# k transposed on VectorE with SBUF transfers in place of TensorE, and seven products reordered in halves of PSUM banks (RWKV-6 attention followed by a GELU MLP)

## The chip, the cores and the metric

One core of a Trainium2 chip. The metric is device microseconds (us) of one execution. A kernel's runs agree within about 0.3% where nothing else is said. In the profile, PE is TensorE's matmuls, PEld its weight loads, DVE is VectorE, ACT ScalarE, SP SyncE; a "q" behind the name is that engine's sequencer, which also issues transfers.

## The reference

```python
# attention: r, k, v, w of (4 batches, 8 heads, 768 steps, 48), u of (8, 48), all float32
for t in range(S):
    cur = u * k[t] (outer) v[t]
    y[t] = r[t] @ (state + cur)
    state = w[t][:, None] * state + k[t] (outer) v[t]
# then, over 3072 rows of 384:
h = x @ w_in                 # 384 x 2048
g = 0.5 * h * (1 + erf(h / sqrt(2)))
out = g @ w_out              # 2048 x 384
```

## The kernel before

The rows are worked through in eight tiles of 384. The MLP of one tile runs on PE while DVE and ACT prepare the attention of the next; attention and MLP are written as generators, and a list says after which step of the MLP each slot of the attention is emitted, which fixes the order on every engine:

```python
    for x in range(1, NX):
        place = ([...] if x == 1 else
                 [0, 1, 4, 10, 14, 16, 17, 18, 20, 22])
        ...
        for step, _ in enumerate(mlp(x - 1)):
            ...
            while place and place[0] <= step:
                place.pop(0)
                next(slots)
```

Three slots of the attention matter. First k, with channels in the partitions and positions in columns, is scaled by DVE (the last of "quarters"). kv needs it the other way round. So it is transposed on PE and copied from PSUM by ACT; then it is the stationary operand (the weights) of 96 small matmuls, "kv", the chunk states:

```python
        for b in range(np_):
            kt_ps = ps.tile([128, 2, BANK], F32, name="kt_ps", tag="d", bufs=3)
            for i in range(NI):
                o = (i % N3) * 128
                nc.tensor.transpose(kt_ps[:, i // N3, o:o + 128], k[:, (b * NI + i) * 128:(b * NI + i + 1) * 128], ident)
            kt = kx[...].rearrange("p (i g d) -> p i g d", g=2, d=G)
            nc.scalar.copy(out=kt.rearrange(...), in_=kt_ps[:, :, 0:N3 * 128])
            kts.append(kt)
        yield
        ...
                        nc.tensor.matmul(kv_ps[half[g], p, i * D:(i + 1) * D], lhsT=kts[b][half[p], i, g, :],
                                         rhs=vs(b, i, g)[half[p], 0:D], start=True, stop=True)
```

On the MLP's side, the second layer is done in seven products of half blocks (16 steps, in place of eight), each of eight matmuls of 192 columns that the trace counts as 16. The first leaves p1, which four others need:

```python
            o1, o2 = psum(), psum()                          # a bank each, two banks in all
            product(o1, of_blocks(0, 0), of_w(0, 0), True)
            nc.scalar.copy(out=p1, in_=o1)
            yield                                            # here: the transposes of k
            product(o1, of_blocks(0, 1), of_w(1, 0))         # goes on adding into o1
            nc.scalar.copy(out=o_sb[0][:, 0:HM], in_=o1)
            yield                                            # here: kv
            product(o2, of_sums(s2), of_t(1), True)
            nc.vector.tensor_add(u2, o2, p1)
            yield
            # ... four more products
```

Of the kernel before, what the change touches and what calls it, by code (L numbers as in the profile page):

```python
# [10 lines left out]
F32 = mybir.dt.float32  # L11
# [10 lines left out]
G = 64  # L22
D = 48
T = 384
Q = 2
NC = T // C
N3 = NC // 2
NI = Q * N3
LEVELS = (1, 2, 4, 8, 16, 32)
QUARTERS = (1, 4, 16)  # L30
BANK = 512
PIECE = 768
AHEAD = 5
SHARES = 8
HALFWAY = 2


# [5 lines left out]
def kernel(  # L43
# [25 lines left out]
    nc = tc.nc  # L69
# [16 lines left out]
    ps = ctx.enter_context(tc.tile_pool(name="ps", bufs=1, space=PSUM))  # L86
# [186 lines left out]
    def attention(x, unit):  # L273
# [6 lines left out]
        n_u = qs * T  # L280
# [50 lines left out]
        def halves():  # L331

            for h in LEVELS:
# [27 lines left out]
                    copy_diagonal(diag)  # L361
                yield

        def quarters():



            n_c = 2 * NI * np_
            rx = kx.rearrange("p (n x) -> p n x", n=n_c)

            def views(h):
                m = C // 4 // h
                r4 = r.rearrange("p (n m four j) -> p n m four j", m=m, four=4, j=h)
                t4 = tot[h].rearrange("p (n m four) -> p n m four", m=m, four=4)
                ends = (0, 3 * C // 4, 5 * C // 4, 6 * C // 4)
                return m, r4, t4, *(rx[:, :, i:j].rearrange("p n (m x) -> p n m x", m=m) for i, j in zip(ends, ends[1:]))

            def plain(h):
                m, r4, t4, s0, s1, s2 = views(h)
                for z, f in ((s0[:, :, :, 0:h], 1), (s1[:, :, :, 0:h], 2), (s2, 3)):  # L380
                    nc.scalar.copy(out=z, in_=r4[:, :, :, f, :])  # L381

            def lay_out(h):
                m, r4, t4, s0, s1, s2 = views(h)
                z = s1[:, :, :, h:]
                nc.vector.tensor_mul(z, r4[:, :, :, 3, :], t4[:, :, :, 2:3].to_broadcast(z.shape))
                nc.vector.tensor_mul(s0[:, :, :, h:], s1, t4[:, :, :, 1:2].to_broadcast(s1.shape))

            diag = diagonal()
            plain(1)  # L390
            lay_out(1)
            copy_diagonal(diag)
            yield
            for h in QUARTERS:
                m, r4, t4, s0, s1, s2 = views(h)
                ds = []
                for n in range(0, np_ * NI, 4):
                    d = ps.tile([128, 2, BANK], F32, name="d", tag="d", bufs=3)
                    for i in range(4):
                        for g in range(2):  # L400
                            for p in range(2):
                                nc.tensor.matmul(d[half[p], g, i * 3 * C // 2:(i + 1) * 3 * C // 2],  # L402
                                                 lhsT=kc[half[g], (n + i) // NI, (n + i) % NI, p],
                                                 rhs=rx[half[g], 2 * (n + i) + p], start=True, stop=True)
                    ds.append(d[:, :, 0:4 * 3 * C // 2].rearrange("p g (n x) -> p g n x", n=4))
                z = r4[:, :, :, 1:, :].rearrange("p n m b j -> p n m (b j)")
                nc.vector.tensor_mul(z, s0, t4[:, :, :, 0:1].to_broadcast(z.shape))
                if h < QUARTERS[-1]:
                    plain(4 * h)
                k4 = k.rearrange("p (n four j) -> p n four j", four=4, j=h)  # L410
                z = k4[:, :, 0:2, :].rearrange("p n b j -> p n (b j)")
                t2 = tot[2 * h].rearrange("p (n two) -> p n two", two=2)
                nc.vector.tensor_mul(z, z, t2[:, :, 1:2].to_broadcast(z.shape))  # L413
                z = k4.rearrange("p n (b two) j -> p n b two j", two=2)[:, :, :, 0, :]
                tz = t4.rearrange("p n m (b two) -> p (n m) b two", two=2)[:, :, :, 1:2]
                nc.vector.tensor_mul(z, z, tz.to_broadcast(z.shape))
                if h < QUARTERS[-1]:
                    lay_out(4 * h)
                for n, d in enumerate(ds):
                    an = at[:, :, 4 * n:4 * n + 4].rearrange("p g n (m x) -> p g n m x", m=m)  # L420
                    o = 0
                    for a in range(3):
                        w_q = (3 - a) * C // 4
                        mask = quarter[h][a].rearrange("p (m x) -> p m x", m=m).unsqueeze(1).unsqueeze(1)
                        data = d[:, :, :, o:o + w_q].rearrange("p g n (m x) -> p g n m x", m=m)
                        nc.vector.copy_predicated(out=an[:, :, :, :, (a + 1) * h:], mask=mask.to_broadcast(data.shape), data=data)  # L426
                        o += w_q
                yield

        yield from halves() if x < 2 else quarters()  # L430


        kts = []
        for b in range(np_):
            kt_ps = ps.tile([128, 2, BANK], F32, name="kt_ps", tag="d", bufs=3)
            for i in range(NI):
                o = (i % N3) * 128
                nc.tensor.transpose(kt_ps[:, i // N3, o:o + 128], k[:, (b * NI + i) * 128:(b * NI + i + 1) * 128], ident)  # L438
            kt = kx[:, parts[b] * Q * T:(parts[b] + 1) * Q * T].rearrange("p (i g d) -> p i g d", g=2, d=G)
            nc.scalar.copy(out=kt.rearrange("p (b i) g d -> p b (i g d)", b=2), in_=kt_ps[:, :, 0:N3 * 128])  # L440
            kts.append(kt)
        yield

        def vs(b, i, g):
# [4 lines left out]
        for b in range(np_):  # L449
            kv_ps = ps.tile([128, 2, BANK], F32, name="kv_ps", tag="d", bufs=3)  # L450
            for i in range(NI):
                for p in range(2):
                    for g in range(2):
                        nc.tensor.matmul(kv_ps[half[g], p, i * D:(i + 1) * D], lhsT=kts[b][half[p], i, g, :],  # L454
                                         rhs=vs(b, i, g)[half[p], 0:D], start=True, stop=True)
            kvs.append(kv_ps[:, :, 0:NI * D].rearrange("p c (q i e) -> p q i c e", q=Q, e=D))
        yield
# [89 lines left out]
    def mlp(x):  # L547
# [34 lines left out]
        if halves:  # L582
            def product(o, lhs, rhs, start=False):
                for j in range(HF):
                    nc.tensor.matmul(o, lhsT=lhs(j), rhs=rhs(j), start=start and j == 0, stop=(j == HF - 1),  # L585
                                     skip_group_check=True)

            def of_sums(s):
                return lambda j: s[j // FG][:, j % FG, :]

            def of_t(i):
                return lambda j: sums[i][:, j, :]

            def of_blocks(a, b):
                return lambda j: block(a, b, j)

            def of_w(b, c):
                return lambda j: w_out_sb[:, b * HF + j, c * HM:(c + 1) * HM]

            def psum():  # L600
                return ps.tile([128, BANK], F32, name="o_ps", tag="mm", bufs=2)[:, 0:HM]

            o_sb = [wk.tile([128, DM], F32, name="o_sb", bufs=2) for _ in range(2)]
            p1, u2, u3 = (wk.tile([128, HM], F32, name=name, bufs=1) for name in ("p1", "u2", "u3"))
            o1, o2 = psum(), psum()
            product(o1, of_blocks(0, 0), of_w(0, 0), True)
            nc.scalar.copy(out=p1, in_=o1)  # L607
            yield
            product(o1, of_blocks(0, 1), of_w(1, 0))
            nc.scalar.copy(out=o_sb[0][:, 0:HM], in_=o1)  # L610
            yield
            product(o2, of_sums(s2), of_t(1), True)
            nc.vector.tensor_add(u2, o2, p1)  # L613
            yield
            o3 = psum()
            product(o3, of_sums(s1), of_t(0), True)
            for k in range(2):

                nc.vector.tensor_sub(s2[k], gs[k + 2][:, :, 0:128], s2[k])
            yield  # L620
            product(o2, of_sums(s3), of_t(2))
            nc.vector.tensor_add(u3, o2, p1)
            nc.vector.tensor_add(o_sb[1][:, HM:], o3, u3)
            yield
            product(o2, of_blocks(1, 1), of_t(3))
            nc.vector.tensor_add(o_sb[1][:, 0:HM], o2, p1)
            store(1, o_sb[1])
            yield
            product(o3, of_sums(s2), of_w(1, 1))
            nc.vector.tensor_add(o_sb[0][:, HM:], o3, u2)  # L630
            store(0, o_sb[0])
            yield

# [58 lines left out]
    for x in range(1, NX):  # L692

        place = ([1, 2, 4, 7, 9, 11, 13, 15, 17, 20, 24, 32] if x == 1 else
                 [0, 1, 4, 10, 14, 16, 17, 18, 20, 22])
        loads = load(x + 1, nc.scalar if x > 1 else nc.sync)
        if x > 1:
            slots = attention(x, 0)
# [78 lines left out]
```

## Time and profile before

| | before |
|---|---|
| median of the runs (us) | 647.65 (646.46 to 648.92) |
| profiled span, mean granted clock of PE | 645.7 us, 0.999 |
| PE busy | 98% |
| one tile, on PE's chain | 74.6 to 74.8 us |
| transposes of k / kv, per tile | 1.31 / 1.54 us |

The lines that carry this are in the prediction below. One group is added here, kv's weight loads. The columns are the line, engine, operation, operands and count, then busy time in us and the mean ns of one, then the idle time before it.

```profile
L454 PEld LDWEIGHTS kv_ps<-v_in,kx 64*64 64x64 f32 x768 | 12.0, 135 | 3.4 <-issue 2.2 <-ACT kx L440 1.2
```

The reader is to keep two things: the mean granted clock is 0.999 (what is missing from 1 lies in the last microsecond), and a weight load of kv takes 135 ns.

### The profile page before, as it was taken

To read this page: it belongs to the slowest core of one execution; us is meant where nothing else is said; L and a number is where in the kernel's file an instruction comes from. 1 tells how busy PE (TensorE), PEld (TensorE's weight loads), DVE (VectorE), ACT (ScalarE), POOL (GpSimd) and SP (SyncE) were. 2 spreads that over 40 slices of the span, in tenths; PEclk is the share of its full clock that TensorE was granted. 3 is DMA by queue.
4 is the path that set the end of the run, shared out by engine and by line. 5 is a ranking of instruction groups with operands and counts; after the bars stand their busy time and mean duration, and the time that the engine had idled before them with its cause. 6 is when DMAs were issued, how large, how long until landed. Compare 5 with 4: busy or idle time off the path is not lost.

```text
span 645.7 us, 17490 instructions
## 1 busy us (share of the span) xinstructions
PE 629.8 (98%) x7918; PEld 451.5 (70%) x7937; DVE 382.1 (59%) x718; ACT 183.4 (28%) x338; POOL 5.6 (1%) x20
## 2 busy tenths in 40 slices
PE   7799998999999999999999999999999999999997
PEld 4566665566796668966697667966698667975695
DVE  8988999747951676428761579426763478500120
ACT  2236465243202521043212432034311422122200
POOL 3000000000000000000000000000000000000000
PEclk9999999999999999999999999999999999999999
DMA  4586346115001240005101240013301000010000
GB/s 160 168 289 208 116 166 250 35 50 141 9 3 47 76 111 2 29 20 130 56 2 36 68 131 2 14 35 93 93 2 36 13 1 2 2 35 13 0 1 37
DMA packets 20409, 43.26 MB, mean 67 GB/s; under 512 B 2672, under 2 KB 6512, under 8 KB 20336
## 3 DMA queue, kind: packets, MB, share of 16 engines
q1 hardware_dynamic: 13344, 26.97, 12.3%
q10 hardware_dynamic: 6992, 15.18, 8.8%
q8 instruction: 62, 1.02, 0.7%
q14 instruction: 11, 0.09, 0.0%
HBM read 36.24 MB, written 4.72 MB: 63 GB/s over the span
## 4 chain that ended last, share of the span: by engine, by line
PE 87%; DVE 9%; issue 2%; DMA 1%; ACT 1%; SPq 0%; DVEq 0%
PE h_ps L567 35%; PE o_ps L585 20%; PE o_ps L639 14%; PE d L402 6%; PE d L316 3%; DVE rkw_in L351 2%; PE y_ps L504 2%; PE y_ps L486 2%; PE kv_ps L454 2%; DVE e L265 1%; PE kt_ps L438 1%; PE warm L167 1%; DVE a_sb L359 1%; DMA rkw_in<-in_rkw_dram 1%; DVE w_out_sb L269 1%
## 5 line engine op out<-in xcount | busy, mean ns | idle before, releaser
L567 PE MATMUL h_ps<-xT,w_in_sb 128*128 128x384 f32 x768 | 257.4, 490 | 0.0
L567 PEld LDWEIGHTS h_ps<-xT,w_in_sb 128*128 128x128 f32 x768 | 143.3, 190 | 96.5 <-ACT xT L517 0.4
L569 ACT ACTIVATE g<-h_ps 128x384 f32<-128x384 f32 x128 | 62.8, 490 | 208.6 <-PE h_ps L567 208.6
L639 PE MATMUL o_ps<-w_out_sb,g 128*128 128x384 f32 x320 | 106.2, 489 | 0.0
L639 PEld LDWEIGHTS o_ps<-w_out_sb,g 128*128 128x128 f32 x320 | 59.9, 190 | 40.4 <-DVE o_sb L645 0.6
L426 DVE COPY_PREDICATED a_sb<-quarter,d 128x384 f32<-128x384 uint8 x162 | 82.6, 552 | 3.7
L645 DVE COPY o_sb<-o_ps 128x384 f32<-128x384 f32 x10 | 5.6, 558 | 87.1 <-PE o_ps L639 87.1
L585 PE MATMUL o_ps<-t,s 128*128 128x192 f32 x336 | 56.4, 328 | 0.0
L585 PEld LDWEIGHTS o_ps<-t,s 128*128 128x128 f32 x336 | 54.5, 190 | 0.3
L402 PEld LDWEIGHTS d<-kx,rkw_in 64*64 64x64 f32 x1728 | 36.4, 133 | 9.8 <-issue 6.5
L402 PE MATMUL d<-kx,rkw_in 64*64 64x96 f32 x1728 | 39.8, 245 | 0.0
L585 PE MATMUL o_ps<-w_out_sb,g 128*128 128x192 f32 x224 | 38.8, 327 | 0.4 <-ACT p L607 0.4
L585 PEld LDWEIGHTS o_ps<-w_out_sb,g 128*128 128x128 f32 x224 | 36.6, 190 | 2.6 <-ACT p L607 0.7
L520 ACT COPY ysb<-y_ps 128x384 f32<-128x384 f32 x8 | 3.8, 476 | 121.0 <-PE y_ps L504 121.0
L381 ACT COPY kx<-rkw_in 128x384 f32<-128x384 f32 x54 | 31.1, 644 | 24.4 <-PE d L402 20.2
L413 DVE TENSOR_TENSOR rkw_in<-rkw_in,tot_sb 128x768 f32<-128x768 f32 x18 | 17.2, 956 | 31.6 <-PE d L402 31.6
L316 PEld LDWEIGHTS d<-rkw_in 64*64 64x64 f32 x1152 | 18.7, 135 | 12.0 <-issue 6.1
L577 DVE TENSOR_TENSOR s<-g 128x512 f32<-128x512 f32 x14 | 9.6, 685 | 28.9 <-ACT g L569 28.9
L517 ACT COPY xT<-y_ps 48x384 f32<-48x384 f32 x46 | 21.7, 473 | 14.8 <-issue 12.3
L316 PE MATMUL d<-rkw_in 64*64 64x64 f32 (+1 forms) x1152 | 21.3, 221 | 4.6 <-DVE rkw_in L351 1.6
L613 DVE TENSOR_TENSOR u<-o_ps,p 128x192 f32<-128x192 f32 x7 | 2.5, 358 | 35.2 <-PE o_ps L585 35.2
L167 PE MATMUL warm<-zeros 128*128 128x512 bf16 x62 | 20.7, 421 | 2.7 <-ACT zeros L162 2.3
(80 smaller groups left out, 568.4 us busy)
## 6 DMA issues: line engine op xcount, KB each, us to landing
rkw_in<-in_rkw_dram ACTq DMA_DIRECT2D x40, 288.0 KB, 2.8
raw<-in_w_out_dram SPq DMA_DIRECT2D x8, 768.0 KB, 4.4
raw<-in_w_in_dram SPq DMA_DIRECT2D x7, 768.0 KB, 6.8
rkw_in<-in_rkw_dram SPq DMA_DIRECT2D x16, 288.0 KB, 5.6
out_dram<-o_sb SPq DMA_DIRECT2D x24, 192.0 KB, 1.9
v_in<-in_v_dram ACTq DMA_DIRECT2D x5, 584.0 KB, 3.9
v_in<-in_v_dram SPq DMA_DIRECT2D x3, 584.0 KB, 7.7
rkw_in<-in_rkw_dram SPq DMA_DIRECT2D x2, 768.0 KB, 5.5
```

The lines of the kernel that those rows point to most:

```text
L167: nc.tensor.matmul(t, lhsT=zeros[:, 0:128], rhs=zeros, start=True, stop=True)
L316: nc.tensor.matmul(d[half[p], g, n * width:(n + 1) * width], lhsT=kc[half[g], b, i, p], rhs=right(half[g], b, i, p), start=True, stop=True)
L351: nc.vector.tensor_mul(rk, rk, tt)
L381: nc.scalar.copy(out=z, in_=r4[:, :, :, f, :])
L402: nc.tensor.matmul(d[half[p], g, i * 3 * C // 2:(i + 1) * 3 * C // 2], lhsT=kc[half[g], (n + i) // NI, (n + i) % NI, p], rhs=rx[half[g], 2 ...
L413: nc.vector.tensor_mul(z, z, t2[:, :, 1:2].to_broadcast(z.shape))
L426: nc.vector.copy_predicated(out=an[:, :, :, :, (a + 1) * h:], mask=mask.to_broadcast(data.shape), data=data)
L517: copy(out=xT[s, pair, :].rearrange("p (i c t) -> p c i t", c=2, t=C), in_=y[s])
L567: nc.tensor.matmul(h_ps, lhsT=w_in_sb[:, f // FI, j, f % FI * 128:(f % FI + 1) * 128], rhs=xT[:, j, :], start=(j == 0), stop=(j == NJ - 1))
L569: nc.scalar.activation(out=gs[group][:, f % FG], in_=h_ps, func=AF.Gelu)
L585: nc.tensor.matmul(o, lhsT=lhs(j), rhs=rhs(j), start=start and j == 0, stop=(j == HF - 1), skip_group_check=True)
L639: nc.tensor.matmul(o, lhsT=block(i, f // HF, f % HF), rhs=w_out_sb[:, f, :], start=(f == 0), stop=(f == NF - 1))
```

## The change

From the third tile on (x of 2 or more; the first two differ) k is not transposed on PE. DVE transposes it in blocks of 32 by 32; the four blocks on the diagonal of the 4 by 4 grid of blocks are copied by ACT, the twelve others are moved by transfers between SBUF places, eight issued by SP and four by ACT. The weights of kv are then read with a step: a row's 12 numbers for one channel lie together, so one weight column is 48 bytes from the next. The intent is to take the twelve transposes (1.31 us per tile) off PE, which is the bound. The products are put in another order, in four half banks, so that five of the seven, in place of three, start afresh and do not add into what another has left; this is aimed at the two waits of the last tile. The list of places is shifted to fit.

```diff
+NC_SP = 8
+        kb, kt_q = (z.rearrange("p (a x) -> p a x", a=4) for z in (kx[:, 0:n_u], w))
+        moves = [(z, (z + i) % 4) for i in (1, 2, 3) for z in range(4)]
+        def move_block(dma, src, dst):
+            dma.dma_start(out=kt_q[dst * 32:(dst + 1) * 32, src, :], in_=kb[src * 32:(src + 1) * 32, dst, :])
+        def blocks_of_k():
+            k32 = k.rearrange("p (n a j) -> p n a j", a=4, j=32)
+            for dst in range(4):
+                nc.vector.transpose(out=kb[:, dst, :].rearrange("p (j n) -> p n j", j=32), in_=k32[:, :, dst, :])
+            for move in moves[:NC_SP]:
+                move_block(nc.sync, *move)
 # ... in the last of the quarters, between scaling k and the predicated copies:
+                    blocks_of_k()
+                    yield
 # ... in place of the transposes, for x >= 2:
+            for z in range(4):
+                nc.scalar.copy(out=kt_q[z * 32:(z + 1) * 32, z, :], in_=kb[z * 32:(z + 1) * 32, z, :])
+            for move in moves[NC_SP:]:
+                move_block(nc.scalar, *move)
+            def k_t(b, i, p, g):
+                return kt_q[half[p], 2 * g:2 * g + 2, :].rearrange("p a (j n) -> p (a j) n", j=32)[:, :, b * NI + i]
 # ... kv:
-  lhsT=kts[b][half[p], i, g, :]
+  lhsT=k_t(b, i, p, g)
 # ... products:
-            o1, o2 = psum(), psum()
+            o1, o4 = psum(), psum()
+            (o1, o2), (o3, o4) = ((o[:, 0:HM], o[:, BANK // 2:BANK // 2 + HM]) for o in (o1, o4))
             product(o1, of_blocks(0, 0), of_w(0, 0), True)
             nc.scalar.copy(out=p1, in_=o1)
             yield
-            product(o1, of_blocks(0, 1), of_w(1, 0))
-            nc.scalar.copy(out=o_sb[0][:, 0:HM], in_=o1)
-            # ... six products into o1, o2, o3, a bank each
+            product(o2, of_blocks(0, 1), of_w(1, 0), True)
+            nc.vector.tensor_add(o_sb[0][:, 0:HM], o2, p1)
+            yield
+            product(o4, of_blocks(1, 1), of_t(3), True)
+            yield
+            # ... four more, into o3, o1, o3, o1 (the last two add into what is there)
-                 [0, 1, 4, 10, 14, 16, 17, 18, 20, 22])
+                 [0, 1, 4, 10, 14, 15, 18, 18, 20, 22])
```

More of the change, by code (lines that the diff above doesn't have):

```diff
@@ L405, in quarters @@
                     ds.append(d[:, :, 0:4 * 3 * C // 2].rearrange("p g (n x) -> p g n x", n=4))
+                last = h == QUARTERS[-1]
                 z = r4[:, :, :, 1:, :].rearrange("p n m b j -> p n m (b j)")
                 nc.vector.tensor_mul(z, s0, t4[:, :, :, 0:1].to_broadcast(z.shape))
-                if h < QUARTERS[-1]:
+                if not last:
                     plain(4 * h)
@@ L416, in quarters @@
                 nc.vector.tensor_mul(z, z, tz.to_broadcast(z.shape))
-                if h < QUARTERS[-1]:
+                if not last:
                     lay_out(4 * h)
+                else:
+                    blocks_of_k()
+                    yield
                 for n, d in enumerate(ds):
@@ L427, in quarters, with k_t @@
                         o += w_q
-                yield
+                if not last:
+                    yield
         yield from halves() if x < 2 else quarters()
-        kts = []
-        for b in range(np_):
-            kt_ps = ps.tile([128, 2, BANK], F32, name="kt_ps", tag="d", bufs=3)
-            for i in range(NI):
-                o = (i % N3) * 128
-                nc.tensor.transpose(kt_ps[:, i // N3, o:o + 128], k[:, (b * NI + i) * 128:(b * NI + i + 1) * 128], ident)
-            kt = kx[:, parts[b] * Q * T:(parts[b] + 1) * Q * T].rearrange("p (i g d) -> p i g d", g=2, d=G)
-            nc.scalar.copy(out=kt.rearrange("p (b i) g d -> p b (i g d)", b=2), in_=kt_ps[:, :, 0:N3 * 128])
-            kts.append(kt)
+        if x < 2:
+            kts = []
+            for b in range(np_):
+                kt_ps = ps.tile([128, 2, BANK], F32, name="kt_ps", tag="d", bufs=3)
+                for i in range(NI):
+                    o = (i % N3) * 128
+                    nc.tensor.transpose(kt_ps[:, i // N3, o:o + 128], k[:, (b * NI + i) * 128:(b * NI + i + 1) * 128], ident)
+                kt = kx[:, parts[b] * Q * T:(parts[b] + 1) * Q * T].rearrange("p (i g d) -> p i g d", g=2, d=G)
+                nc.scalar.copy(out=kt.rearrange("p (b i) g d -> p b (i g d)", b=2), in_=kt_ps[:, :, 0:N3 * 128])
+                kts.append(kt)
+            def k_t(b, i, p, g):
+                return kts[b][half[p], i, g, :]
+        else:
+            for z in range(4):
+                nc.scalar.copy(out=kt_q[z * 32:(z + 1) * 32, z, :], in_=kb[z * 32:(z + 1) * 32, z, :])
+            for move in moves[NC_SP:]:
+                move_block(nc.scalar, *move)
+            def k_t(b, i, p, g):
+                return kt_q[half[p], 2 * g:2 * g + 2, :].rearrange("p a (j n) -> p (a j) n", j=32)[:, :, b * NI + i]
         yield
@@ L453, in attention @@
                     for g in range(2):
-                        nc.tensor.matmul(kv_ps[half[g], p, i * D:(i + 1) * D], lhsT=kts[b][half[p], i, g, :],
+                        nc.tensor.matmul(kv_ps[half[g], p, i * D:(i + 1) * D], lhsT=k_t(b, i, p, g),
                                          rhs=vs(b, i, g)[half[p], 0:D], start=True, stop=True)
@@ L600, in psum @@
             def psum():
-                return ps.tile([128, BANK], F32, name="o_ps", tag="mm", bufs=2)[:, 0:HM]
+                return ps.tile([128, BANK], F32, name="o_ps", tag="mm", bufs=2)
             o_sb = [wk.tile([128, DM], F32, name="o_sb", bufs=2) for _ in range(2)]
             p1, u2, u3 = (wk.tile([128, HM], F32, name=name, bufs=1) for name in ("p1", "u2", "u3"))
-            o1, o2 = psum(), psum()
+            o1, o4 = psum(), psum()
+            (o1, o2), (o3, o4) = ((o[:, 0:HM], o[:, BANK // 2:BANK // 2 + HM]) for o in (o1, o4))
             product(o1, of_blocks(0, 0), of_w(0, 0), True)
@@ L608, in mlp @@
             yield
-            product(o1, of_blocks(0, 1), of_w(1, 0))
-            nc.scalar.copy(out=o_sb[0][:, 0:HM], in_=o1)
+            product(o2, of_blocks(0, 1), of_w(1, 0), True)
+            nc.vector.tensor_add(o_sb[0][:, 0:HM], o2, p1)
             yield
-            product(o2, of_sums(s2), of_t(1), True)
-            nc.vector.tensor_add(u2, o2, p1)
+            product(o4, of_blocks(1, 1), of_t(3), True)
             yield
-            o3 = psum()
-            product(o3, of_sums(s1), of_t(0), True)
+            product(o3, of_sums(s2), of_t(1), True)
+            nc.vector.tensor_add(u2, o3, p1)
+            yield
+            product(o1, of_sums(s1), of_t(0), True)
+            nc.scalar.copy(out=o_sb[1][:, HM:], in_=o1)
             for k in range(2):
@@ L620, in mlp @@
             yield
-            product(o2, of_sums(s3), of_t(2))
-            nc.vector.tensor_add(u3, o2, p1)
-            nc.vector.tensor_add(o_sb[1][:, HM:], o3, u3)
-            yield
-            product(o2, of_blocks(1, 1), of_t(3))
-            nc.vector.tensor_add(o_sb[1][:, 0:HM], o2, p1)
+            product(o3, of_sums(s3), of_t(2))
+            nc.vector.tensor_add(u3, o3, p1)
+            nc.vector.tensor_add(o_sb[1][:, 0:HM], o4, u3)
+            nc.vector.tensor_add(o_sb[1][:, HM:], o_sb[1][:, HM:], u3)
             store(1, o_sb[1])
             yield
-            product(o3, of_sums(s2), of_w(1, 1))
-            nc.vector.tensor_add(o_sb[0][:, HM:], o3, u2)
+            product(o1, of_sums(s2), of_w(1, 1))
+            nc.vector.tensor_add(o_sb[0][:, HM:], o1, u2)
             store(0, o_sb[0])
```

## The prediction

> **What bounds the kernel now.** I read the page first: busy shares, then the chain of work that ended last.
>
> ```profile
> PE 629.8 (98%) x7918; PEld 451.5 (70%) x7937; DVE 382.1 (59%) x718; ACT 183.4 (28%) x338; POOL 5.6 (1%) x20
> ...
> PE 87%; DVE 9%; issue 2%; DMA 1%; ACT 1%; SPq 0%; DVEq 0%
> ```
>
> TensorE (PE) carries 87% of the chain; the 9% of VectorE (DVE) lie in the first 106 us, which the change doesn't touch. The chain in order of time then shows a period of about 74.6 us per tile with almost no wait. This is the stretch of one tile that the change rewrites:
>
> ```profile
> 243.23 2.14 PE d L402 x96
> 245.37 2.13 PE h_ps L567 x6
> 247.50 2.60 PE o_ps L585 x16
> 250.10 1.31 PE kt_ps L438 x12
> 251.41 2.60 PE o_ps L585 x16
> 254.01 1.54 PE kv_ps L454 x96
> 255.56 8.00 PE o_ps L585 x48
> ```
>
> Each piece begins where the last ended, so a microsecond taken off PE here is a microsecond of the kernel, and so is one of PE waiting. kt_ps (twelve transposes of k) is what the change removes. The timeline of the same stretch shows what the others do meanwhile:
>
> ```profile
> 245.82 0.95 DVE L413 TENSOR_TENSOR rkw_in<-rkw_in,tot_sb 128x768 f32<-128x768 f32 x1
> 246.80 0.96 DVE L416 TENSOR_TENSOR rkw_in<-rkw_in,tot_sb 128x768 f32<-128x768 f32 x1
> ...
> 247.34 2.76 PE L585 MATMUL o_ps<-w_out_sb,g 128*128 128x192 f32 x16
> 247.54 0.49 ACT L569 ACTIVATE g<-h_ps 128x384 f32<-128x384 f32 x1 [3.78 <-PE h_ps L567]
> 247.68 4.01 DVE L426 COPY_PREDICATED a_sb<-quarter,d 128x384 f32<-128x384 uint8 x9
> ...
> 249.94 1.47 PE L438 MATMUL kt_ps<-ident,rkw_in 128*128 128x128 f32 x12
> 250.14 0.32 ACT L607 COPY p<-o_ps 128x192 f32<-128x192 f32 x1 [2.11 <-PE o_ps L585]
> ```
>
> Two things matter. DVE has finished scaling k (L416) only at 247.76, while PE is through its first product at 249.94. And ScalarE (ACT) copies that product out of PSUM (L607, "p1") at 250.14 at once, hidden behind the transposes on PE. In the last tile, which has no attention beside it, nothing hides it:
>
> ```profile
> 614.99 0.32 ACT L607 COPY p<-o_ps 128x192 f32<-128x192 f32 x1 [2.11 <-PE o_ps L585]
> ...
> 615.36 2.87 PE L585 MATMUL o_ps<-w_out_sb,g 128*128 128x192 f32 x16 [0.41 <-ACT p L607]
> ...
> 626.48 2.87 PE L585 MATMUL o_ps<-t,g 128*128 128x192 f32 x16 [0.45 <-DVE u L622]
> ```
>
> The second product waits for p1 (0.41 us), and a later one for a DVE read (0.45 us). The reordering of the products aims at these. Last, what a transfer between SBUF places costs the engine that issues it, and what stepped operands cost:
>
> ```profile
> 272.64 2.41 SPq L524 DMA_DIRECT2D xT<-ysb  x4
> 272.65 1.42 ACTq L524 DMA_DIRECT2D xT<-ysb  x2
> 274.10 0.96 ACT L517 COPY xT<-y_ps 48x384 f32<-48x384 f32 x2 [1.49 <-issue]
> ```
>
> ```profile
> L381 ACT COPY kx<-rkw_in x9: 506/512/923, 213.3 to 236.2; 128x384 f32<-128x384 f32 x9
> ...
> L386 DVE TENSOR_TENSOR kx<-rkw_in,tot_sb x2: 550/550/551, 223.3 to 237.2; 128x384 f32<-128x384 f32 x2
> ...
> L386 DVE TENSOR_TENSOR kx<-rkw_in x1: 871/871/871, 213.3 to 213.3; 128x384 f32<-128x384 f32 x1
> ```
>
> Two issues held ACT for 1.42 us, 0.7 each, and the next copy could not start ("issue"). The slow forms of L381 and L386 are those of h = 1, whose reads step 16 bytes.
>
> **What the Trainium skill says.**
> (1) The Trainium skill, "PSUM — Partial Sum Buffer", section "PSUM bank collisions raise a hardware error": two engines must be kept apart by bank and quadrant, "not by address". So putting o1 and o2 into halves of one bank does not free PE from waiting for ACT's read of o1. The built instructions agree: the first matmul of the changed second product waits for exactly the ACT copy p1. The before-trace has only the same-address case (0.41 us).
> (2) The Trainium skill, "DMA: Bandwidth & Descriptors", section "Issuing engines are not separate DMA queues": issuing from several engines only saves sequencer time, "usually small relative to the DMA itself". The trace is less kind: 0.54 to 0.84 us of ACT per issue, beside 1.9 to 2.2 us to landing.
> (3) The Trainium skill, "SBUF — State Buffer", the note on SBUF cachelines under "Door 1: The DMA port swizzle": 16-byte lines, a penalty where each access goes to a new line. The 512 to 923 ns and 550 to 871 ns above agree. The changed kernel writes its transposes and reads k as weights in steps of 48 bytes.
> (4) The Trainium skill, "TensorE: Matmul & The Clock Gate", "What's actually happening": PE's clock falls to half after an idle window of about 3.4 us. No place in the before-trace shows it (granted clock 0.999).
>
> **The change part by part**, on the clock of the stretch above; six tiles (the third to the eighth) have it.
>
> Removed: 12 transposes, 1.31 us of PE per tile, all on the path; two ACT copies of 0.80 us, not on the path.
>
> Added on DVE: four 32x32-block transposes of 128x384 each, in front of the nine predicated copies. A 384-element DVE instruction takes 0.55 us contiguous and 0.87 us stepped; I take 0.65 as an estimate between them. They start after L416, at 247.76, so the fourth ends near 247.76 + 4 x 0.65 = 250.4.
>
> Added on ACT, in this order by the built instructions: after the last Gelu (ends 248.0), four copies of 32x384, each waiting for its transpose; then four transfers; then p1. The fourth copy can be dispatched at 250.4, and the transfers are issued behind it: 4 x 0.69 (the mean of 0.54 and 0.84; SP issues its eight at the same time) = 2.8 us, until 253.2. Then p1 takes 0.32 and the handovers some 0.1: 253.6.
>
> On PE: the first product still ends at 249.94, with no transposes behind it now. The second waits for p1 until 253.6: 3.6 us idle, where before there was none. This is the term that decides. Net per tile: +3.6 - 1.31 = +2.3 us.
>
> Transfers: kv waits for all twelve. The eighth of SP waits, by a reused semaphore, for the first of ACT (issued 250.4, landed about 252.6), so it starts near 253 and lands near 255.5. kv comes at 253.6 + two products of 2.6 = 258.8. Hidden, with 3 us to spare, only because of the stall; without it kv would stand at 249.94 + 5.2 = 255.1 and just touch it.
>
> kv itself: 96 weight loads and matmuls in 1.54 us, now with weights stepped 48 bytes. If loading them takes double, near 2.5 us; no stepped weight load is in the trace. I give it even odds: +0.5 us per tile.
>
> The state updates on DVE span 4.1 us (258.74 to 262.84) and have 5.2 us of products behind kv: hidden. The predicated copies end some 5 us after the transposes and the second group of sums (2 us), near 257: before kv.
>
> Products: seven remain, of the same length. Of the last tile's two waits the 0.45 goes, the 0.41 stays. In tiles with attention there was nothing to win.
>
> Sum: 6 x (2.3 + 0.5) - 0.5 = +16; I shade it to +14.5, as the slow and the fast side of the issue time are not alike. 647.5 + 14.5 = 662 us.
>
> **The rivals.**
> (a) The plain reading: PE is the bound and loses 6 x 1.31 = 7.9 us, perhaps a little more: 639. For it: 98% busy, the chain. Against it: the p1 wait behind ACT's transfers, built into the order. It needs ACT's issues to be nearly free, which the 1.49 us of "issue" denies.
> (b) The same stall with cheap parts: transposes 0.53 each (249.9) and issues of 0.334, as the 288 KB loads of the same ACT queue take in the trace. p1 ends at 249.9 + 1.3 + 0.4 = 251.6: 1.7 us idle, net +0.4 per tile: 650.
> (c) The stall with dear parts: transposes 0.87 (251.2), issues 0.75: p1 at 254.6, 4.7 us idle, net +3.4; with slow weights +1.0 more: 6 x 4.4 = 26, so 674. An idle stretch of that length could also drop PE's clock, (4) above, which adds perhaps 1.7 us per tile (3.4 us at half rate): 680 or more.
> (d) The wait for the transfers in front of kv takes over from p1: only if p1 is early. The total would be near (b).
>
> **Range and chances.** The floor of the stall is well supported (order, 247.76, 249.94); its size hangs on transposes and issues that no row shows in this form. Range 651 to 674. The 2% line lies at 660.5, just under my 662: slower 0.57, within 2% 0.40, faster 0.03.
>
> **What would show it.** In the changed profile: the idle time before the o_ps matmuls of the second product, released by ACT p1, 3.6 us six times and about 0.4 in the last tile; four transposes of 0.55 to 0.87 us after L434 (old L416); four ACT transfer issues of about 0.7 us just ahead of p1; no wait of PE for DMA before kv; kv 1.54 us or up to 2.5; no kt in the tiles from the third on. I am wrong if PE goes from product to product without a gap (then rival a), if the gap stands before kv and is released by a DMA (d), or if the clock row falls below 9.

## The result, and the profile after

| | before | after |
|---|---|---|
| median (us) | 647.65 (646.46 to 648.92) | 688.23 (687.91 to 690.24) |
| profiled span (us) | 645.7 | 686.1 |
| mean granted clock | 0.999 | 0.973 |
| one tile on the chain (us) | 74.6 to 74.8 | 81.9 |

The changed kernel takes 1.0633 of the time before (95% interval 1.0604 to 1.0662), and the predicted range of 651 to 674 does not hold it. Here and below a ratio is the mean time of one kernel's runs over that of the other's in the same rounds, so it is not quite the ratio of the medians.

From the page: busy shares, the granted clock, and the engines on the chain that ended last.

```profile
PE 651.6 (95%) x7865; PEld 470.1 (69%) x7865; DVE 402.2 (59%) x749; ACT 187.2 (27%) x350; POOL 5.7 (1%) x20
...
PEclk9999999999999998999989998999989999899999
...
PE 73%; DVE 21%; issue 2%; DMA 1%; ACT 1%; ACTq 0%; DVEq 0%
```

PE is busy for 22 us more although 72 transposes are gone, and it has more idle time besides. VectorE's share of the chain has gone from 9% to 21%: the chain now leaves PE in every tile. The clock row has an 8 in five places. A slice is 17 us long, so an 8 is not a slightly slower clock over the slice; it is a few microseconds at half speed.

The timeline of the same stretch of the same tile (start in us, duration, engine, line; in brackets the idle time before and what ended it). Line numbers have shifted by some 35: L620 is the product that was L585, L644 is p1, and the last scaling of k by DVE has ended at 253.16.

```profile
252.73 2.76 PE L620 MATMUL o_ps<-w_out_sb,g 128*128 128x192 f32 x16
...
253.19 2.90 DVE L376 STREAM_TRANSPOSE kx<-rkw_in 128x384 f32<-128x384 f32 x4
...
256.13 2.49 ACTq L371 DMA_DIRECT2D rkw_in<-kx  x4
...
258.65 0.32 ACT L644 COPY p<-o_ps 128x192 f32<-128x192 f32 x1 [2.03 <-DMA rkw_in<-kx]
...
259.03 5.49 PE L620 MATMUL o_ps<-w_out_sb,g 128*128 128x192 f32 x16 [3.53 <-ACT p L644]
```

The first product has ended at 255.33 (252.73 + 2.60, the time from one product to the next; its modelled end is 255.49). DVE's four transposes follow the scaling, ACT's four issues follow the last transpose (with one copy of a block at 256.12), p1 follows the issues, and the second product follows p1 at 259.03. The predicted stall is there. It is also there in the list of waits (in all, times, longest): 22.0 us in seven waits, of which the last tile's is 0.4, so 21.6/6 = 3.6 us per tile.

```profile
PE o_ps L620 <- ACT p L644: 22.0, 7, 3.8
```

But look at the second product itself: 5.49 us, where before it took 2.77. The chain goes on:

```profile
259.03 8.23 PE o_ps L620 x32
267.26 3.37 PE kv_ps L489 x96
```

Two products took 8.23 us in place of 5.2, and kv 3.37 in place of 1.54. No wait is in either. The reason for the first is in the windows: the same stretch, cut into pieces of 3.41 us at whose edges the clock changes. Columns are the window and its length, busy time of PE with the number of matmuls, the granted clock, the DMA share and GB/s.

```profile
254.43:257.85 3.42, 1.07 (x7) 1.00 0.21 58
257.85:261.26 3.41, 2.23 (x7) 0.50 0.43 115
261.26:264.67 3.41, 3.41 (x13) 0.50 0.00 0
264.67:268.09 3.42, 3.42 (x44) 1.00 0.00 0
```

PE stops at 255.33 (255.49 by the modelled end); some 2.5 us later, at 257.85, the clock falls to half and stays there for 6.83 us, until 264.67, although PE works again from 259.03 on. In this tile that cost 8.23 - 5.47 = 2.8 us, after an idle time of 3.7 us. Five of the six tiles show 6.83 us at half clock behind the stall, the other 3.41, half of that. The reason for kv's length is in its group of weight loads:

```profile
L489 PEld LDWEIGHTS kv_ps<-v_in,rkw_in 64*64 64x64 f32 x576 | 19.9, 233 | 1.4 <-issue 1.4
```

One load takes 233 ns, with steps of 48 bytes, against 135 before.

The sum over the six tiles: the stall 21.6 us; the two products behind it take 7.15, 8.23, 8.25, 8.24, 8.26 and 8.39 us, 48.5 in all, where at full clock they take 5.47 (measured in the first experiment), so 48.5 - 6 x 5.47 = 15.7 us by the clock; kv 6 x (3.38 - 1.54) = 11.0 us; against that 6 x 1.31 = 7.9 us of transposes gone, and 0.45 us of the last tile. 21.6 + 15.7 + 11.0 - 7.9 - 0.45 = 40.0, and the spans differ by 686.1 - 645.7 = 40.4 us.

### The profile page after: what moved, and what is told of

It reads as the page before. It is cut to its first block, busy times and chain, and to the rows that moved or that the text cites. A ratio compares the mean times of both kernels' runs of the same rounds, so it can differ in the third digit from the quotient of the medians.

```text
span 686.1 us, 17538 instructions
## 1 busy us (share of the span) xinstructions
PE 651.6 (95%) x7865; PEld 470.1 (69%) x7865; DVE 402.2 (59%) x749; ACT 187.2 (27%) x350; POOL 5.7 (1%) x20
## 4 chain that ended last, share of the span: by engine, by line
PE 73%; DVE 21%; issue 2%; DMA 1%; ACT 1%; ACTq 0%; DVEq 0%
PE h_ps L602 24%; PE o_ps L620 19%; PE o_ps L676 14%; PE d L418 4%; DVE a_sb L447 3%; PE kv_ps L489 3%; PE d L317 3%; DVE kx L376 3%; PE warm L168 2%; DVE rkw_in L352 2%; PE y_ps L539 2%; PE y_ps L521 2%; DVE rkw_in L434 2%; DVE rkw_in L431 2%; DMA rkw_in<-kx 1%
## 5 line engine op out<-in xcount | busy, mean ns | idle before, releaser
L676 PEld LDWEIGHTS o_ps<-w_out_sb,g 128*128 128x128 f32 x320 | 59.9, 190 | 40.4 <-DVE o_sb L682 0.6
L620 PE MATMUL o_ps<-w_out_sb,g 128*128 128x192 f32 x224 | 54.2, 412 | 22.0 <-ACT p L644 22.0
L620 PEld LDWEIGHTS o_ps<-w_out_sb,g 128*128 128x128 f32 x224 | 50.2, 248 | 25.9 <-ACT p L644 24.0
L620 PE MATMUL o_ps<-t,s 128*128 128x192 f32 x336 | 58.0, 330 | 0.0
L620 PEld LDWEIGHTS o_ps<-t,s 128*128 128x128 f32 x336 | 54.3, 190 | 0.7
L655 ACT COPY o_sb<-o_ps 128x192 f32<-128x192 f32 x7 | 2.2, 318 | 112.5 <-PE o_ps L620 62.2
L506 DVE TENSOR_TENSOR st<-st,kv_ps 128x96 f32<-128x96 f32 x80 | 17.5, 251 | 17.3 <-PE kv_ps L489 15.8
L612 DVE TENSOR_TENSOR s<-g 128x512 f32<-128x512 f32 x14 | 9.5, 680 | 28.9 <-ACT g L604 28.9
L168 PE MATMUL warm<-zeros 128*128 128x512 bf16 x81 | 22.9, 403 | 2.3 <-ACT zeros L163 2.3
```

What stands on the lines that cost most here:

```text
L168: nc.tensor.matmul(t, lhsT=zeros[:, 0:128], rhs=zeros, start=True, stop=True)
L620: nc.tensor.matmul(o, lhsT=lhs(j), rhs=rhs(j), start=start and j == 0, stop=(j == HF - 1), skip_group_check=True)
L676: nc.tensor.matmul(o, lhsT=block(i, f // HF, f % HF), rhs=w_out_sb[:, f, :], start=(f == 0), stop=(f == NF - 1))
```

## The experiments

The theory: three costs, each with its own cause. (A) PE stalls because p1 stands behind transposes and transfer issues on ACT. (B) The stall drops PE's clock. (C) Stepped weights make kv slower. Rivals: the clock drop has another cause (DVE's or the transfers' load, say); the transfers themselves, or the order of the products, cost the time. All kernels computed the right result. Runs of 3 rounds stand beside runs of the kernel before on the same chip.

| run | what is altered | median us (range) | ratio to before (95%) |
|---|---|---|---|
| e1_warm | after, PE kept busy in the stall | 678.82 (675.53 to 680.13) | 1.0467 (1.0437 to 1.0497) |
| e2_swap | after, third product before the second | 659.35 (658.81 to 663.34) | 1.0188 (1.0158 to 1.0218) |
| e3_stepped | before, weights of kv stepped | 661.02 (658.30 to 662.50) | 1.0195 (1.0167 to 1.0224) |
| e4_products | before, new products alone | 647.05 (645.53 to 647.38) | 0.9978 (0.9961 to 0.9994) |
| e5_p1_first | after, p1 ahead of ACT's issues | 659.04 (656.71 to 660.29) | 1.0174 (1.0147 to 1.0200) |
| e6_contig | after, weights contiguous | 668.12 (663.67 to 668.92) | 1.0304 (1.0266 to 1.0342) |
| e7_all_sp | after, all transfers issued by SP | 678.19 (671.05 to 679.47) | 1.0451 (1.0394 to 1.0508) |
| e9_repaired | after, contiguous, swapped, kv later | 641.95 (641.38 to 642.92) | 0.9915 (0.9900 to 0.9929) |
| e8_best | e9, ACT copies in place of transfers | 638.12 (637.31 to 638.32) | 0.9856 (0.9838 to 0.9874) |

**e1_warm: keep PE busy while it waits.** Fifteen matmuls on zeros go into a bank that is not in use at that time; they change no result and leave the wait in place.

```diff
+            bank4 = o4
 # ...
             nc.scalar.copy(out=p1, in_=o1)
+            if x < NX - 1:
+                for _ in range(15):
+                    nc.tensor.matmul(bank4, lhsT=zeros[:, 0:128], rhs=zeros, start=True, stop=True)
             yield
```

> The changed kernel with 15 dummy matmuls (zeros, 128x512, some 0.216 us each, 3.2 us together) between the first and the second product of the six tiles that have attention beside them; they write the other bank and wait for nothing that p1 holds. Theory A (the loss is a stall of PE at p1 of 3.6 us, then PE at half clock behind it, then stepped weight loads): the second product still starts when p1 is done, but the clock row stays at 1.0 and the second and third product take 2.6 us each again instead of 8.2 together: 5 tiles x 2.9 + about 1.5 in the first = 16 us less, so near 672 us; kv still 3.4 us. Rival R1 (the slow products come from the transfers or ACT contending for SBUF, not from the clock): they stay slow, time stays near 688. Rival R2 (kv is slow because of the clock too): kv falls to about 1.6 us and the time to near 661.

It took 678.82 us, 9.4 less than the changed kernel, where the clock's whole 15.7 were expected. The timeline of one tile:

```profile
336.55 3.40 PE L648 MATMUL o_ps<-zeros 128*128 128x512 bf16 x15
...
340.50 2.87 PE L620 MATMUL o_ps<-w_out_sb,g 128*128 128x192 f32 x16 [0.55 <-ACT p L645]
...
349.27 7.15 PE L620 MATMUL o_ps<-t,s 128*128 128x192 f32 x32
```

The second product is back at 2.87 us, so theory B holds: doing nothing useful, but being busy, keeps the clock. The second product still starts late, 340.50 - 336.55 = 4.0 us after the first has ended (the stall of the changed kernel was 3.7), nothing of DVE, ACT or the transfers was altered, and only PE's idleness was gone. The missing 6 us are in the last line: two products behind kv took 7.15 us in place of 5.40, at a half clock that starts right behind kv. That happened in three tiles (about 5 us), and PE's time in the stall is 0.3 longer in six (about 2). The changed kernel has no drop behind kv. So C also costs clock, by the look of it; e3 tests that by itself.

**e3_stepped: the kernel before with stepped weights.** The transposes stay on PE; ACT only writes them so that kv reads with 48-byte steps.

```diff
-            kt = kx[...].rearrange("p (i g d) -> p i g d", g=2, d=G)          # for all x; now only for x < 2
+                kt = kx[:, 0:n_u].rearrange("p (g d n) -> p n g d", g=2, d=G)[:, b * NI:(b + 1) * NI]
+                for z in range(2):
+                    nc.scalar.copy(out=kt[:, z * N3:(z + 1) * N3].rearrange("p i g d -> p i (g d)"),
+                                   in_=kt_ps[:, z, 0:N3 * 128].rearrange("p (i y) -> p i y", i=N3))
```

> The kernel before, with TensorE's transposes, in which only the layout of the copied k is changed in the six tiles from the third on: the 64 weights of kv are stepped by 48 bytes as in the changed kernel, not contiguous. No transfers, no stall, clock full. Theory A (stepped weight loads cost 1.8 us a tile): kv 3.4 us in place of 1.54, 6 x 1.84 = 11 us more, near 658.5 us, unless the ACT copies into the stepped layout (perhaps 1.5 us each) make kv wait as well, then up to 664. Rival R2 (kv was slow only because of the clock or the transfers in flight): kv stays at 1.6 us, time 647 to 650.

It took 661.02 us, 13.1 more than before. Of the chain of one tile:

```profile
332.98 3.41 PE kv_ps L460 x96
336.39 9.52 PE o_ps L591 x48
```

kv takes 3.41 us with no DVE transposes, no transfers and no stall in the kernel: 6 x (3.38 - 1.54) = 11.0 us belong to the steps alone (the six tiles take 3.37 to 3.41 us). In this tile the three products behind it take 9.52 us where they took 8.00 before. The windows of PE alone around kv's end (busy, clock):

```profile
335.00:336.00 1.00, 1.00 (x38) 1.00 0.00 0
336.00:337.00 1.00, 1.00 (x14) 0.52 0.09 16
```

The clock falls at 336.04, just before kv ends, although PE's row is busy 100% of both windows. In the profiled run that was so in two tiles. It is not in every tile, and how many differs between runs (the fastest run, 658.30 us, has a mean clock of 0.999), so its size should not be taken as fixed. Which tiles it hits is taken up under "Why the prediction was wrong".

**e2_swap: the third product before the second.** o4 lies in the other bank, so this product need not wait for ACT's read of o1.

```diff
+            product(o4, of_blocks(1, 1), of_t(3), True)
+            yield
             product(o2, of_blocks(0, 1), of_w(1, 0), True)
             nc.vector.tensor_add(o_sb[0][:, 0:HM], o2, p1)
             yield
-            product(o4, of_blocks(1, 1), of_t(3), True)
-            yield
```

> The changed kernel with the second and third product exchanged, so that the one that writes the other bank (o4) comes right behind the first and the one that shares o1's bank (o2) comes third. Theory A: o4 needs no p1 and fills 2.6 us of the 3.6 us stall; about 1.0 us of it stays, too short for the clock to drop: 6 x 2.6 + 16 = 31 us less, near 657 us, kv still 3.4 us. Rival R3 (PE waits for ACT in general, or for the transfers, and not for p1 by the bank): o4 waits just as long, time near 688.

It took 659.35 us, 28.9 less than the changed kernel, for an exchange of two calls. The waits of this kernel:

```profile
PE o_ps L620 <- ACT p L644: 6.8, 6, 1.2
```

The profiled run was the slowest of the four (663.3), with a half clock behind kv in three tiles, as in e1. The stall is 6.8/6 = 1.1 us, one product (2.6) shorter, and the half clock behind it is gone. What is left over the kernel before is mostly kv's 11.0. It shows that the stall was a matter of bank order: nothing on ACT or DVE got faster.

**e5_p1_first: p1 ahead of the copies and issues on ACT.** The slot with ACT's work on k comes one step later.

```diff
-                 [0, 1, 4, 10, 14, 15, 18, 18, 20, 22])
+                 [0, 1, 4, 10, 14, 16, 18, 18, 20, 22])
```

> The changed kernel with one number altered: ACT's four block copies and four transfer issues come after p1 and not ahead of it (slot 16 in place of 15). Theory A (the stall is ACT's order): p1 is ready 0.4 us after the first product, the 3.6 us stall and the half-clock stretch behind it vanish; what takes its place is a wait of PE before kv for the last transfer (lands some 261.5 to 262 on the changed kernel's clock, kv ready at 261): about 1 us. Stepped kv stays 3.4 us, and with a half-clock window behind kv in some tiles as the last runs showed: near 661 us. Rival R5 (the transposes on VectorE and the transfers cost as such, whatever the order on ACT): near 688.

It took 659.04 us, 29.2 less than the changed kernel, by another way than e2. The wait for p1 is now 2.9 us in seven. The chain of one tile:

```profile
329.76 5.47 PE o_ps L620 x32
335.23 0.39 PE kv_ps L489 x2
335.62 0.08 issue
335.70 3.69 PE kv_ps L489 x93
```

The two products run at full clock, and the slow kv stays. At the start of kv half a microsecond passes (0.39 and 0.08) in which PE waits for a transfer: with the stall gone, kv comes just too early, as rival (d) of the prediction had it, but the wait is small (the list of waits has 0.5 us, in one tile). Behind kv the clock falls in two tiles of the profiled run.

**e4_products: the new products alone, on the kernel before.** The diff is the product part of the change and nothing else.

> The kernel before with only the new order of the products in halves of banks; k is transposed by TensorE as before. Theory A: the transposes lie between the first and the second product and hide p1; nothing is won or lost in the tiles with attention, and of the last tile's two waits (0.41 and 0.45 us) the second goes: 647 us, no clock drop. Rival R4 (the halves of banks themselves are the cost, by collisions of PE and the readers in one bank): slower by several us, with longer o_ps products also here.

It took 647.05 us, a ratio of 0.9978. Beside the transposes on PE, p1 is copied while PE is busy, and the bank-wide wait costs nothing; what the order wins is the last tile's 0.45 us, in which PE no longer waits for DVE (the medians differ by 0.9). So the new order of products is harmless by itself; the stall comes with the loss of the transposes that hid p1. The order before would not have avoided it: its second product adds into o1 and waits for p1 as well (0.41 us in the last tile, in the prediction's lines). DVE's transposes with the order before were not run.

**e6_contig: contiguous weights.** DVE writes its transposes without steps, and the copies and transfers put each block where the weights of one matmul lie together. The transfers' pieces become 128 bytes.

```diff
+        kt_n = w.rearrange("p (n a j) -> p n a j", a=4, j=32)
-            dma.dma_start(out=kt_q[dst * 32:(dst + 1) * 32, src, :], in_=kb[src * 32:(src + 1) * 32, dst, :])
+            dma.dma_start(out=kt_n[dst * 32:(dst + 1) * 32, :, src, :], in_=kb[...].rearrange("p (n j) -> p n j", j=32))
-                nc.vector.transpose(out=kb[:, dst, :].rearrange("p (j n) -> p n j", j=32), in_=k32[:, :, dst, :])
+                nc.vector.transpose(out=kb[:, dst, :].rearrange("p (n j) -> p n j", j=32), in_=k32[:, :, dst, :])
-                return kt_q[half[p], 2 * g:2 * g + 2, :].rearrange("p a (j n) -> p (a j) n", j=32)[:, :, b * NI + i]
+                return kt_n[half[p], b * NI + i, 2 * g:2 * g + 2, :].rearrange("p a j -> p (a j)")
```

> The changed kernel with the blocks laid out so that VectorE writes its transposes without a step and TensorE loads kv's 64 weights without a step; in exchange each transfer moves 12 runs of 128 bytes per partition in place of one of 1536. Theory A: transposes 0.55 us each in place of 0.84 (the step is what made them long), kv 1.54 us in place of 3.4, no half-clock window behind kv. If the issues still take 0.6 us, the stall at p1 is 3.0 us in place of 3.6, at the edge of dropping the clock: 657 with no drop, 673 with one in each tile. Rival R6: the short runs make the transfers land later, and PE waits for DMA before kv, by more than 1 us per tile.

It took 668.12 us, 20.1 less than the changed kernel. The groups of transposes and of kv's loads:

```profile
L377 DVE STREAM_TRANSPOSE kx<-rkw_in 128x384 f32<-128x384 f32 x24 | 11.7, 546 | 0.2
...
L490 PEld LDWEIGHTS kv_ps<-v_in,rkw_in 64*64 64x64 f32 x576 | 8.9, 135 | 1.4 <-issue 1.4
```

The load is back at 135 ns and kv at 1.54 us: theory C from the other side. A transpose without steps takes 546 ns, where the changed kernel's took 838, so the stall shrinks too, to (18.0 - 0.4)/6 = 2.9 us. That is still enough to drop the clock in five of the six tiles, by one or two windows of 3.41 us. The fastest of the runs (663.67) has the highest clock, 0.989 against 0.985 to 0.987, so a part of the spread of 5 us is clock. A stall need not last 3.4 us to cost clock, and one of 2.9 us need not cost any.

**e7_all_sp: all twelve transfers issued by SP.** ACT issues none, so p1 follows the four copies.

```diff
-NC_SP = 8
+NC_SP = 12
```

> The changed kernel with all twelve transfers issued by SP and none by ACT. Theory A (ACT's four issues of 0.63 us hold p1): the stall falls from 3.6 to about 1.2 to 1.7 us, and what ends it is p1 behind the block copies; SP needs 12 x 0.62 = 7.5 us to issue, so that kv now waits for a transfer, about 2 us. Stepped kv 3.4 us stays. Per tile -1.3 + 1.5 + 2 + 1.8 = +4: near 672 us with no clock drop, up to 684 with some. Rival: if issues on ACT do not matter, the stall stays at 3.6 us and the time at 688 or above.

It took 678.19 us, 10.0 less than the changed kernel. The stall in front of the second product is (9.6 - 0.4)/6 = 1.5 us. But the chain now goes another way: transposes, twelve issues one after the other on SP (0.63 us each), the last transfer, kv:

```profile
342.49 1.91 DMA rkw_in<-kx
...
344.44 3.43 PE kv_ps L489 x90
```

The wait has moved from p1 to kv (2.4 us in five waits, and kv is stretched besides, as its last matmuls wait for the last transfers), and PE's clock falls there too, in five of six tiles: the mean granted clock is 0.980. Taking work off ACT was right and giving it to SP was not: the issues form a queue wherever they stand.

**e9_repaired: e6 and e2 together, kv later.** This asks whether the transfers are slow as such. It and e8 were timed in 5 rounds.

```diff
-                 [0, 1, 4, 10, 14, 15, 18, 18, 20, 22])
+                 [0, 1, 4, 10, 14, 15, 19, 19, 21, 22])
```

> The changed kernel's own idea, transfers included (eight by SP, four by ACT ahead of p1), with three repairs: o4 as second product, no steps in the transposes and in kv's weights (transfers of 12 runs of 128 bytes), kv after the fourth product. Theory A (the transfers are not slow in themselves; what cost was whom they held up): the transposes end near 255.4 on the changed kernel's clock, ACT's issues near 258, p1 near 258.2, the third product is ready at 257.9 and waits some 0.3 us; the last transfer lands near 261.5, kv stands at 263.4 and does not wait. Per tile -1.31 + 0.3, and 0.5 us in the last: near 641 us, no clock drop. Rival R7 (transfers between SBUF places cost as such, by contention with the engines' reads): kv waits for DMA or other engines' instructions get longer, 646 us or more.

It took 641.95 us, less than the kernel before by 0.85%, with the same transfers and the same DVE transposes as e6. kv is 1.54 us, the wait for p1 is 2.1 us in six, PE does not wait for a transfer in front of kv, and the mean granted clock is 1.000. So neither the transfers nor the block transposes on DVE explain the loss of themselves. It came from the stall that they caused by standing ahead of p1, its clock, and the steps.

**e8_best: no transfers at all.** ACT copies between quadrants of 32 partitions by itself: sixteen copies in place of four copies and twelve transfers, in two slots.

```diff
-            for z in range(4):
-                nc.scalar.copy(out=kt_n[z * 32:(z + 1) * 32, :, z, :], in_=kb[z * 32:(z + 1) * 32, z, :]...)
-            for move in moves[NC_SP:]:
-                move_block(nc.scalar, *move)
+            for dst in range(4):
+                for src in range(4):
+                    nc.scalar.copy(out=kt_n[dst * 32:(dst + 1) * 32, :, src, :],
+                                   in_=kb[src * 32:(src + 1) * 32, dst, :].rearrange("p (n j) -> p n j", j=32))
+                if dst == 0:
+                    yield
-                 [0, 1, 4, 10, 14, 15, 19, 19, 21, 22])
+                 [0, 1, 4, 10, 14, 15, 16, 19, 19, 21, 22])
```

> A version meant to beat both: no transfers at all; VectorE transposes without a step, ScalarE moves all sixteen blocks by copies from one group of 32 partitions to another (16 x 0.5 us, four ahead of p1 and twelve behind it), o4 as second product, kv after the fourth product with weights without a step. Theory A: the 1.31 us of transposes leave TensorE in six tiles (7.9 us) and 0.5 us in the last, no stall above some tenths, clock at 1.0: near 639.5 us, ratio 0.987. If the sixteen copies take longer than 0.5 us each, kv waits for ACT: then 642 to 650.

It took 638.12 us, a ratio of 0.9856: it beats both kernels. The chain of one tile is PE alone again:

```profile
318.86 10.40 PE o_ps L621 x64
329.26 1.54 PE kv_ps L490 x96
```

Four products run without a gap in 10.40 us (4 x 2.60), and kv follows. 647.3 - 638.1 = 9.2 us: 6 x 1.31 = 7.9 of transposes, 0.45 and 0.4 of the last tile (with o4 second, its wait for p1 is gone too), and the rest is within what runs differ by. This is what the change was meant to win. ACT, with 27% to 28% of its time busy in both kernels, had room for 96 copies of 0.51 us.

## Why the prediction was wrong

The direction and the mechanism were foreseen; the size was not: 662 was predicted, with 651 to 674 as the range, and 688 came. Step by step, per tile:

| term of the sum | predicted (us) | measured (us) | holds? |
|---|---|---|---|
| second product waits for p1 | +3.6 | +3.6 | yes |
| transposes gone | -1.31 | -1.31 | yes |
| kv with stepped weights | +0.5 | +1.84 | no, too small |
| clock behind the stall | 0 (rival (c): +1.7) | +2.6 | no, left out |
| last tile, once | -0.45 | -0.45 | yes |

- The stall: right, with its cause (the bank-wide wait for ACT's read, and ACT's issues ahead of p1) and its length. Two errors in its working cancelled: a transpose starts every 0.73 us, not 0.65, and an issue took 0.63, not 0.69; that the sum came out at 3.6 is luck in part.
- "An idle stretch of that length could also drop PE's clock ... which adds perhaps 1.7 us per tile": this is the step that failed. It was written down as part of a rival, with a total outside the range, while the sum had a stall of 3.6 us and nothing for the clock. A stall that long should have brought the clock into the sum itself, since the prediction knew of the rule and had no reason to think it would not act. It was also under-sized: the half clock lasted 6.83 us in five tiles of six, not 3.4, and cost 15.7 us in all. e1 shows that PE's idleness is the cause: with PE kept busy in the same wait, the product behind it takes 2.87 us.
- "I give it even odds: +0.5 us per tile": the second term that failed. The effect was certain, not even, and twice as large as the case that was weighed: 3.4 us, not 2.5. e3 shows it alone, e6 shows it undone. 6 x (1.84 - 0.5) = 8 us.
- These two make 15.7 + 8.0 = 24 us of the 26 by which 688.2 exceeds 662; the rest is the 1.5 us by which the prediction shaded its sum of +16, and rounding.
- No DMA wait in front of kv: right for the changed kernel, and the reason given ("only because of the stall") is confirmed by e5 (0.5 us) and e7 (the wait moves to kv).
- Rival (a), 639, was judged to need nearly free issues. e8 reaches 638.1 in another way: with the issues gone, the bank order mended and the weights contiguous.
- The prediction named a sign that it was wrong, a clock row below 9, and that sign came: five slices show 8.

Why the clock falls in one tile and not in the next can be read from the traces. In each of the eleven, all changes of the clock lie whole multiples of 3.413 us apart, so it looks to be set anew for each window of that length. First e6, two tiles with the same stall of 2.9 us (PE alone; columns as above):

```profile
253.78:257.19 3.41, 2.10 (x13) 1.00 0.19 31
257.19:260.60 3.41, 1.77 (x11) 1.00 0.86 128
260.60:264.02 3.42, 3.42 (x23) 1.00 0.09 14
...
332.29:335.70 3.41, 0.46 (x3) 1.00 0.68 104
335.70:339.11 3.41, 3.41 (x11) 0.50 0.46 69
```

Where the stall is split between two windows, PE is busy for 52% or more of each and the clock stays; where it falls into one, PE is busy for 13% of it and the next window is at half clock. From the third tile on, with the last two windows of each trace left out, the eleven windows with PE busy for 13% to 33% were followed by half clock, and none with 52% or more was, those with stepped weights left out; between 33% and 52% there is none. Full clock came back only after a window in which PE was busy throughout; 65% to 82% did not bring it back. Then kv with its stepped weights in e3, two tiles (busy time of kv's instructions alone, on PE, PEld and DVE):

```profile
332.63:336.04 3.41, 3.13 (x92) 3.13 (x96) 0.00 (x0) 1.00 0.00 0
336.04:339.45 3.41, 0.35 (x12) 0.19 (x8) 0.00 (x0) 0.50 0.03 5
489.64:493.05 3.41, 3.01 (x92) 2.89 (x88) 0.00 (x0) 1.00 0.02 5
493.05:496.47 3.42, 0.00 (x0) 0.00 (x0) 0.41 (x2) 1.00 0.00 0
```

kv lasts about as long as a window. In the changed kernel, e1, e2, e3 and e5 the ten windows of which kv filled 92% or more were followed by half clock, and none with 89% or less. In the changed kernel kv filled at most 82%, which fits its having no drop there. What stays open: in e7, where kv is interrupted by waits, shares of 50% to 70% were enough in three tiles; in the first 106 us windows with PE busy for about half went either way; and no run moved a stall or kv against the windows on purpose, so this is a pattern of these traces and not a tested rule.

## What to carry to other kernels

Ask of every instruction that is removed from the bounding engine what it was hiding; here the transposes covered a PSUM copy, and without them the bounding engine stood behind another engine's queue. A stall of a few microseconds on TensorE has to be counted with the clock that it costs afterwards, which here was most of the stall again, and a layout that suits the transfer may be paid by each weight load. Where the order of two products in different banks can be exchanged, that is the cheapest repair: two calls exchanged won 29 of the 40 us.

## What the Trainium skill lacked or had wrong

- "TensorE: Matmul & The Clock Gate", section "What's actually happening", gives half clock after an idle window of about 3.4 us. Here the window need not be idle: PE was busy for 1.07 us of the 3.42 us before the clock fell at 257.85, and for up to 33% of such windows elsewhere; a stall of 2.9 us was enough in five of six tiles of e6. No section gives the share.
- The same page has nothing on slow weight loads and the clock. In e3 the clock fell to half behind 96 stepped weight loads while PE's row was at 1.00 of the window and no gap stood ahead.
- The same page, section "LDWEIGHTS (loading the stationary operand)", makes the time a matter of the number of columns alone. With the same 64 columns in float32, a step of 48 bytes took the load from 135 to 233 ns, and 96 loads and matmuls from 1.54 to 3.4 us. (Item (3) of the prediction foresees a penalty for such steps, without a size.)
- "VectorE: DVE Perf Modes", section "The three transpose paths", has 311 ns for 128x128 in bf16. It has nothing for float32 or stepped output: 128x384 in float32 took 546 ns contiguous and 838 ns with its output stepped by 48 bytes.
- "DMA: Bandwidth & Descriptors", section "Issuing engines are not separate DMA queues", calls the sequencer's time to initiate a DMA usually small. A 48 KB transfer between SBUF places cost 0.63 us of ACT or SP per issue, beside 1.9 us to landing; four of them held p1 back for 2.5 us.
